# One more piece of the maxima beside an output product, and plain steps with one piece less, in a two-attention kernel

## The chip, the cores and the metric

The kernel runs on one core of one Trainium2 chip. The metric is the device time of one execution in microseconds; the number for a kernel is the median of several runs. The engines are TensorE (PE for its matmuls and PEld for its weight loads), VectorE (DVE), ScalarE (ACT), GpSimd (POOL) and the DMA queues, most of which SyncE (SP) issues.

## What is computed

Two attention layers on inputs of their own, both with 2048 positions, width 576, 32 heads of 18 and one projection each for q, k, v and for the output. Layer A looks, at each position, at 8 positions in steps of 2 back; layer B is full attention. The results stand side by side in the output.

```python
# A: W, dil = 8, 2; idx = pos - off, masked where negative
logits = einsum("bhsd,bhswd->bhsw", q, kg) * scale      # kg, vg: the 8 gathered positions
a = einsum("bhsw,bhswd->bhsd", softmax(logits), vg) @ wo_a
# B
scores = einsum("bhqd,bhkd->bhqk", q, k) * scale
b = einsum("bhqk,bhkd->bhqd", softmax(scores), v) @ wo_b
out = concatenate([a, b], axis=-1)
```

## The kernel before

**Projections, then steps.** A first part projects the inputs (and begins with the maxima). The main loop (from L1122) then makes 512 steps, numbered by `step`: 8 groups of 4 heads, in each 4 blocks of 512 queries, in each 16 tiles of 128 keys. The sixth group begins with step 320.

**A step.** For each of the 4 heads a `score` (L222): one matmul of the tile's keys with the block's queries into a PSUM bank (L229), and its exponent on ScalarE (L235). Then `weigh` (L698) multiplies the values with the exponents of the step before into `po` (L700, eight pairs of weight load and matmul to a step); after the last key tile of a block `finish` copies `po` out (L709). Heads 0 and 2 use rows 0 to 63 of the TensorE array, heads 1 and 3 rows 64 to 127. I call the four scores s0 to s3.

**Pieces of the maxima.** The softmax of B needs the largest score of each query before the block's own steps. So the scores are computed twice: ahead of time, in 2048 pieces of 128 queries by 512 keys. A piece is one matmul (`take`, L159) and one reduction on VectorE (`reduce`, L166). Each block of 64 pieces must be done several steps before the block's first score (`AHEAD`); `least`, `turn`, `halve` and `place` carry its result into the queries' rows. `maximum(r)` issues the next piece of row half r, and `given` counts the pieces by half. A score with a piece beside it (`also`) takes the piece from the other row half. I call the pieces beside scores m0 to m3, after their score.

**How many pieces.** A step has three pieces, or four when `behind()` (L1102) finds that blocks would come late; the last steps have none, when all are given. `positions` (L1111) says beside which scores: with three, heads 0, 1, 2 or 0, 1, 3, by which half has had more.

**Product steps.** The outputs of A, and part of those of B, are multiplied by their output weights inside steps of the loop: a function in `inside` is called ahead of the third or fourth score (L1129). It calls `beside` (L987), which runs two chains of matmuls of 288 columns at once, one in each row half (13 or 14 each for A, `halves`, L266), into two banks. Two pieces are put in among them, as long as pieces are left; I call them p1 and p2, and a third one p3. Which later steps count as product steps is known beforehand in `producing`; `behind` uses it. The two sums are joined by ScalarE (a copy, L918) and VectorE (an addition, L919).

**Banks.** There are seven PSUM banks in rings: 0 to 3 are "scores", and 4, 5 and 6 are "else". The pieces take their banks from "else", in turn, by `bank()` (L80); the product takes one bank from each ring. A bank is written again only when its reader has finished. Each engine works its instructions off in the order written.

Of the kernel before, what the change touches and what calls it, by code (L numbers as in the profile page):

```python
# [22 lines left out]
NG = H // 4  # L23
NT = S // 128
NB = S // 512
# [11 lines left out]
PIECES = 2 * 4 * NB  # L37
# [6 lines left out]
GAP = 54  # L44

A_FROM = 10


def ap(t, *dims):
# [10 lines left out]
def two_attentions(ctx: ExitStack, tc, xa, wa, woa, xb, wb, wob, out):  # L60
# [16 lines left out]
    rings = {"all": list(range(7)), "scores": [0, 1, 2, 3], "else": [4, 5, 6]}  # L77
    ring = "all"

    def bank(kind=None):  # L80
        r = rings[kind or ring]
        r.append(r.pop(0))
        return p_bank.tile([128, 512], F32, name=f"bank{r[-1]}")
# [25 lines left out]
    step = 0  # L109
# [4 lines left out]
    def plan(start, pieces):  # L114
        for n, f in pieces:
            agenda[start + n].append(f)

    def due():
        for f in agenda.pop(step, []):
            f()  # L120
# [84 lines left out]
    given = [0, 0]  # L205
    projecting = True

    def maximum(r):

        n, i = divmod(given[r], PIECES)  # L210
        given[r] += 1
        if n not in blocks:
            blocks[n] = block(*divmod(n, NB))
        take, reduce = blocks[n]
        piece = (r, i // 2 // NB, i // 2 % NB, i % 2)
        ps = take(*piece)
        return lambda: reduce(ps, *piece)
# [4 lines left out]
    def score(g, b, kt, h, also, kind="scores"):  # L222

        assert (g, b) in placed
        qs, ks = sets[g % 3]
        p, r = divmod(h, 2)
        ps = bank(kind)
        at = slice(64 * r, 64 * r + 56)
        nc.tensor.matmul(ps, ks[at, p, 128 * kt : 128 * kt + 128], qs[at, b, p], start=True, stop=True)  # L229
        reduce = maximum(1 - r) if also else None  # L230

        counted[0] += 1
        early = counted[0] % 8 < 6
        e = (e_room if early else work).tile([128, 512], F32, name="e", bufs=6 if early else 2)
        nc.scalar.activation(e, ps, AF.Exp, scale=SCALE)  # L235
        if reduce:
            reduce()
        return e
# [100 lines left out]
    with (tc.tile_pool(name="x", bufs=1, side="right") as xp,  # L339
# [104 lines left out]
        if True:  # L444
# [238 lines left out]
            turns = len(work_list) - NT + 4  # L683
# [8 lines left out]
        step = 0  # L692
# [5 lines left out]
    def weigh(g, b, kt, es):  # L698
        for i in range(4):
            nc.tensor.matmul(po[32 * i : 32 * i + 19], vs[g][:, kt, 19 * i : 19 * i + 19], es[i],  # L700
                             start=kt == 0, stop=kt == NT - 1)
        if kt == NT - 1:
            finish(g, b)
# [78 lines left out]
    producing = set()  # L782
# [23 lines left out]
    def local(j):  # L806
# [64 lines left out]
        def weighted(c):  # L871
            if c == 0:
                st["o"] = work.tile([128, DH, SUB], F32, name="ao", bufs=1)
            at = wide()
            nc.gpsimd.tensor_mul(at, ap(st["lg"], (0, 2), (SUB, W), (1, SUB)), window(st["v"], c))  # L875
            nc.gpsimd.tensor_add(at[:, :, :4], at[:, :, :4], at[:, :, 4:])  # L876
            nc.gpsimd.tensor_add(at[:, :, :2], at[:, :, :2], at[:, :, 2:4])
            nc.gpsimd.tensor_add(st["o"][:, 2 * c : 2 * c + 2], at[:, :, 0], at[:, :, 1])
# [28 lines left out]
        def finished(h):  # L907
            inside.append(lambda: sums_of_a(h))

        def sums_of_a(h):  # L910
            his, los = zip(*wo["a"])
            w = his[:4], los[:4], his[4], los[4]
            cols = slice(288 * h, 288 * h + 288)
            if h == 0:
                st["y"] = ys["a", j, st["n"]] = work.tile([128, D], F32, name="y", bufs=4)
            one, two = beside("scores", *(halves(r, 0, w, st["x"], cols, slice(0, 128), True) for r in range(2)))
            y = st["y"][:, cols]
            nc.scalar.activation(y, two, AF.Copy)  # L918
            behind_scores.append(lambda: nc.vector.tensor_add(y, one, y))  # L919
# [6 lines left out]
        for c in range(DH // 2):  # L926
            pieces.append((5 + 5 * c // 2, lambda c=c: match(c)))
            pieces.append((37 + 5 * c // 2, lambda c=c: weighted(c)))
        at = A_FROM + GAP * j - 24

        at = max(at, STEPS * (at // STEPS) + 14) - A_FROM - GAP * j
        for n in range(3):
            pieces.append((at + n if j else n - 7, lambda n=n: arrange(n)))
        for n, (at, ends) in enumerate(((70, (78, 80)), (81, (87, 89)))):
            pieces.append((at, lambda n=n: get(n)))
            for h in range(2):
                pieces.append((ends[h], lambda h=h: finished(h)))
                producing.add(A_FROM + GAP * j + ends[h] + 1)
            pieces.append((ends[1] + 6, lambda n=n: load(out[p0 + 128 * n : p0 + 128 * n + 128, :D], ys["a", j, n])))
# [43 lines left out]
    inside = []  # L983
# [3 lines left out]
    def beside(kind, *both):  # L987

        sums_ = [bank(k)[:, :288] for k in (kind, None)]
        turns = [[(sums_[r], *ab, i == 0, i == len(t) - 1) for i, ab in enumerate(t)] for r, t in enumerate(both)]  # L990
        pair = kind and sum(given) + 2 <= NG * NB * PIECES * 2
        if pair:

            for r in range(2):
                turns[r].insert(6 + 4 * r, None)
        for i in range(max(map(len, turns))):
            for r in range(2):
                if i < len(turns[r]):
                    if turns[r][i]:
                        ps, a, b, start, stop = turns[r][i]  # L1000
                        nc.tensor.matmul(ps, a, b, start=start, stop=stop)  # L1001
                    else:
                        maximum(r)()
        if pair:

            rings["else"].append(rings["else"].pop(0))
        return sums_

    def sum_of(y, t, h, chunks, kind=None):

        pos, cols = slice(128 * t, 128 * t + 128), slice(288 * h, 288 * h + 288)
        both = []
        for r in range(2):
            both.append([])
            for c, (hi, lo) in enumerate(chunks):
                at = slice(64 * r, min(64 * r + 64, hi.shape[0]))
                whi, wlo = wo["b"][c]
                both[r] += [(a[at, pos], w[at, cols]) for a, w in ((hi, whi), (hi, wlo), (lo, whi))]
        one, two = beside(kind, *both)
        nc.vector.tensor_copy(y, one)  # L1020
        nc.vector.tensor_add(y, two, y)
# [59 lines left out]
    for j in range(NJ):  # L1081
        plan(A_FROM + GAP * j, local(j))
    for g in range(1, NG):
# [16 lines left out]
    total = early + rest  # L1100

    def behind():  # L1102

        most = 0
        for n in range(sum(given) // (2 * PIECES), NG * NB):
            until = NT * n - AHEAD
            more = 3 * (until - step) + 2 * sum(step <= p < until for p in producing)
            most = max(most, 2 * PIECES * (n + 1) - sum(given) - more)
        return most

    def positions(n):  # L1111

        if n == 3:
            ahead = given[1] > given[0]
            return (0, 1, 3) if ahead else (0, 1, 2)
        if n == 1:
            return (0,) if given[0] > given[1] else (1,)
        return range(4) if n > 3 else (0, 1) if n == 2 else ()
# [3 lines left out]
    while step < ALL:  # L1122
        n, kt = divmod(step, NT)
        g, b = divmod(n, NB)
        places = positions(min(4 if behind() > 0 else 3, total - sum(given)))
        es = []
        for h in range(4):

            if inside and h == (3 if 3 in places else 2):  # L1129
                inside.pop(0)()  # L1130

            es.append(score(g, b, kt, h, h in places, "else" if step == ALL - 1 and h > 1 else "scores"))
        for fs in (behind_scores, outside):
            while fs:
                fs.pop(0)()
        while waiting:
            waiting.pop(0)()
        if ready:
            weigh(*ready.pop(0))
        ready.append((g, b, kt, es))  # L1140
        due()
        if waiting:
            waiting.pop(0)()
        step += 1
# [26 lines left out]
```

## Time and profile before

| | |
|---|---|
| median of 3 runs | 1646.94 us (1646.8 to 1649.85) |
| the profiled execution | 1648.65 us, its span 1646.9 us |
| PE busy, of the span | 1635.5 us, 99% |
| DVE busy | 1395.2 us, 85% |
| ACT busy | 1222.5 us, 74% |
| POOL busy | 960.6 us, 58% |
| TensorE clock granted | 1.0 |
| the loop's first and last weigh | at 423.6 and 1636 us |

A busy time adds up all the stretches in which an engine works on something. PE's matmuls are pipelined and their ends are modelled, so a PE that is always busy may still wait; the start of a weight load or of a matmul is the sharper mark. In the timeline a row is one instruction, or several of one kind one after the other: start and length in us, engine, line, operation, and behind "idle before" what the engine waited for. A line number is that of the kernel before.

### The profile page before, as it was taken

The numbers are of one execution on the slowest core, as the hardware profiler recorded it, in microseconds if no ns is written. First come the engines' busy times: TensorE is split into PE (matmuls) and PEld (weight loads), VectorE is DVE, ScalarE is ACT, GpSimd is POOL, SyncE is SP. The second block draws the span as 40 slices with busy tenths as digits, with TensorE's granted clock in tenths as the row PEclk, the third lists the DMA queues.
The fourth block names the chain that finished last, engine by engine and source line by source line (L and its number), as shares of the span: only waits on it lengthen the run. The fifth ranks groups of instructions, "written<-read, shape, count | busy, mean of one in ns | idle before, by whom it ended". The sixth has DMA issues, their size and how long they took to land.

```text
span 1646.9 us, 33732 instructions
## 1 busy us (share of the span) xinstructions
PE 1635.5 (99%) x12906; PEld 938.5 (57%) x12906; DVE 1395.2 (85%) x2386; ACT 1222.5 (74%) x2419; POOL 960.6 (58%) x800
## 2 busy tenths in 40 slices
PE   9999999999999999999999999999999999999999
PEld 7999778999433444444344344344444344344676
DVE  5199999999899989889889889899899999898533
ACT  6424432111899998998998998998998998998544
POOL 2406642210095995994994994994995997920000
PEclk9999999999999999999999999999999999999999
DMA  8937955422616346157238225616525132034201
GB/s 235 250 116 204 256 166 139 133 89 90 95 43 105 96 135 123 68 130 137 67 90 155 88 70 143 128 64 123 132 79 117 66 107 78 21 114 136 88 37 59
DMA packets 188353, 188.22 MB, mean 114 GB/s; under 512 B 118384, under 2 KB 132208, under 8 KB 186464
## 3 DMA queue, kind: packets, MB, share of 16 engines
q1 hardware_dynamic: 183328, 174.53, 40.9%
q0 software_dynamic: 4032, 10.63, 3.1%
q8 instruction: 101, 1.65, 0.4%
q10 hardware_dynamic: 832, 0.92, 0.2%
q14 instruction: 60, 0.49, 0.1%
HBM read 113.16 MB, written 88.12 MB: 122 GB/s over the span
## 4 chain that ended last, share of the span: by engine, by line
PE 93%; DMA 4%; ACT 1%; DVE 1%; POOL 0%; issue 0%; SPq 0%; ACTq 0%; POOLq 0%
PE po L700 30%; PE bank L229 25%; PE bank L322 14%; PE bank L159 13%; PE bank L1001 7%; PE bank L259 3%; DMA den<-o 1%; DMA dqk<-olo 1%; DMA dqk<-ohi 1%; DMA first<-wb 1%; DMA raw<-xa 1%; POOL xlo L370 0%; DMA raw<-xb 0%; DMA first<-xb 0%; PE bank L976 0%
## 5 line engine op out<-in xcount | busy, mean ns | idle before, releaser
L166 DVE TENSOR_REDUCE mx<-bank 128x1 f32<-128x512 f32 x2048 | 1286.9, 683 | 145.1 <-PE bank L159 113.7
L235 ACT ACTIVATE e<-bank 128x512 f32<-128x512 f32 x2048 | 1060.2, 613 | 95.0 <-PE bank L229 57.4
L159 PE MATMUL bank<-ks,qs 54*128 54x512 f32 x2048 | 751.0, 423 | 2.5 <-DVE mx L166 2.4
L229 PEld LDWEIGHTS bank<-qs,ks 56*128 56x128 f32 x2048 | 330.0, 185 | 450.2 <-ACT e L235 424.6
L229 PE MATMUL bank<-qs,ks 56*128 56x512 f32 x2048 | 581.5, 425 | 0.0
L700 PE MATMUL po<-e,v 128*19 128x512 f32 x4096 | 539.6, 599 | 0.0
L159 PEld LDWEIGHTS bank<-ks,qs 54*128 54x128 f32 x2048 | 340.6, 184 | 15.8 <-DVE mx L166 8.8
L832 POOL TENSOR_TENSOR pr<-aq,akv 128x1024 f32<-128x1024 f32 x72 | 158.4, 2200 | 28.3 <-DMA akv<-dpart 25.8
L700 PEld LDWEIGHTS po<-e,v 128*19 128x19 f32 x4096 | 69.5, 96 | 179.7 <-issue 169.3
L875 POOL TENSOR_TENSOR pr<-lg,akv 128x1024 f32<-128x1024 f32 x72 | 158.1, 2196 | 0.6
L836 POOL TENSOR_TENSOR pr<-pr 128x1024 f32<-128x1024 f32 x64 | 152.4, 2381 | 5.0
L651 ACT ACTIVATE ohi<-bank 128x512 f32<-128x512 f32 (+1 forms) x56 | 30.5, 595 | 147.3 <-issue 115.7
L322 PE MATMUL bank<-xhi,ahi 64*128 64x512 f32 (+1 forms) x448 | 113.7, 387 | 0.0
L322 PE MATMUL bank<-xhi,alo 64*128 64x512 f32 (+1 forms) x448 | 112.2, 388 | 0.0
L322 PE MATMUL bank<-xlo,ahi 64*128 64x512 f32 (+1 forms) x448 | 110.9, 389 | 0.4 <-POOL xlo L370 0.3
L876 POOL TENSOR_TENSOR pr<-pr 128x512 f32<-128x512 f32 x72 | 92.3, 1282 | 5.6
L370 POOL TENSOR_TENSOR alo<-raw,ahi 128x512 fp32r<-128x512 f32 (+1 forms) x14 | 17.6, 1254 | 120.6 <-ACT ahi L369 86.5
L463 POOL TENSOR_TENSOR olo<-olo,ohi 128x512 fp32r<-128x512 f32 x36 | 46.2, 1295 | 68.3 <-ACT ohi L462 60.8
L322 PEld LDWEIGHTS bank<-xhi,ahi 64*128 64x128 f32 (+1 forms) x448 | 64.6, 181 | 3.7
L322 PEld LDWEIGHTS bank<-xhi,alo 64*128 64x128 f32 (+1 forms) x448 | 63.3, 182 | 3.6
L322 PEld LDWEIGHTS bank<-xlo,ahi 64*128 64x128 f32 (+1 forms) x448 | 62.0, 182 | 5.2 <-POOL xlo L370 1.6
L1001 PE MATMUL bank<-wohi,at 64*128 64x288 f32 x512 | 64.5, 297 | 0.0
(196 smaller groups left out, 1738.5 us busy)
## 6 DMA issues: line engine op xcount, KB each, us to landing
do<-n SPq DMA_DIRECT2D x28, 512.0 KB
da<-ohi SPq DMA_DIRECT2D x52, 256.0 KB
dpart<-da SPq DMA_DIRECT2D x16, 702.0 KB
akv<-dpart SPq DMA_DIRECT2D x16, 702.0 KB
out<-y SPq DMA_DIRECT2D x32, 288.0 KB
qs<-dqk SPq DMA_DIRECT2D x30, 288.0 KB
ks<-dqk SPq DMA_DIRECT2D x30, 288.0 KB
at<-dao SPq DMA_DIRECT2D x64, 128.0 KB
```

The lines of the kernel that those rows point to most:

```text
L159: nc.tensor.matmul(ps, qs[at, b, p, 128 * t : 128 * t + 128], ks[at, p, 512 * k : 512 * k + 512], start=True, stop=True)
L166: nc.vector.tensor_reduce(mx[:, r, p, t, k : k + 1], ps, axis=AX.X, op=ALU.max)
L229: nc.tensor.matmul(ps, ks[at, p, 128 * kt : 128 * kt + 128], qs[at, b, p], start=True, stop=True)
L235: nc.scalar.activation(e, ps, AF.Exp, scale=SCALE)
L259: nc.tensor.matmul(ps, a, b, start=c == i == 0, stop=c == 4 and i == 1)
L322: nc.tensor.matmul(ps, a, b, start=start, stop=stop)
L700: nc.tensor.matmul(po[32 * i : 32 * i + 19], vs[g][:, kt, 19 * i : 19 * i + 19], es[i], start=kt == 0, stop=kt == NT - 1)
L832: nc.gpsimd.tensor_mul(pr, ap(st["q"][:, 2 * c], (SUB, 2), (0, W), (1, SUB)), window(st["k"], c))
L836: nc.gpsimd.tensor_add(st["pr"], st["pr"], pr)
L875: nc.gpsimd.tensor_mul(at, ap(st["lg"], (0, 2), (SUB, W), (1, SUB)), window(st["v"], c))
L876: nc.gpsimd.tensor_add(at[:, :, :4], at[:, :, :4], at[:, :, 4:])
L1001: nc.tensor.matmul(ps, a, b, start=start, stop=stop)
```

## The change

`beside` puts in three pieces instead of two, two of them in the row half that has had fewer, at places 6, 10 and 14 of the chains. While it does, the bank that the product has taken from "else" is held out of that ring, and afterwards it is put back as the last one used. A step with three pieces into which a product falls always has the pieces beside heads 0, 1 and 3, with the product ahead of head 3. From step 328 up to 395 every odd step that is not a product step has two pieces instead of three, and `behind` reckons with all that.

```diff
+TWO_FROM = 5 * NT * NB + 8
+TWO_UNTIL = TWO_FROM + 68
...
-        pair = kind and sum(given) + 2 <= NG * NB * PIECES * 2
-        if pair:
-
-            for r in range(2):
-                turns[r].insert(6 + 4 * r, None)
+        three = kind and sum(given) + 4 <= NG * NB * PIECES * 2
+        if three:
+
+            less = int(given[0] >= given[1])
+            for r, i in ((less, 6), (1 - less, 10), (less, 14)):
+                turns[r].insert(i, None)
+
+            held = rings["else"].pop()
...
-        if pair:
-
-            rings["else"].append(rings["else"].pop(0))
+        if three:
+            rings["else"].append(held)
...
-            more = 3 * (until - step) + 2 * sum(step <= p < until for p in producing)
+            twos = len([p for p in range(max(step, TWO_FROM), min(until, TWO_UNTIL)) if p % 2 and p not in producing])
+            more = 3 * (until - step) - twos + 3 * sum(step <= p < until for p in producing)
...
-        places = positions(min(4 if behind() > 0 else 3, total - sum(given)))
+        two = TWO_FROM <= step < TWO_UNTIL and step % 2 and step not in producing
+        places = positions(min(4 if behind() > 0 else 2 if two else 3, total - sum(given)))
+        if inside and len(places) == 3:
+            places = (0, 1, 3)
...
-            if inside and h == (3 if 3 in places else 2):
+            if inside and h == (3 if len(places) == 3 else 2):
```

## The prediction

> **What bounds the kernel now.** I read the page first, then the groups by line, then the timeline of single steps. A step is one pass of the main loop: four scores (L229, s0 to s3), the pieces of the maxima beside them (L159, m), and one weigh (L700). Here are the page's busy line, its chain that ended last, and two groups by line.
>
> ```profile
> PE 1635.5 (99%) x12906; PEld 938.5 (57%) x12906; DVE 1395.2 (85%) x2386; ACT 1222.5 (74%) x2419; POOL 960.6 (58%) x800
> PE 93%; DMA 4%; ACT 1%; DVE 1%; POOL 0%; issue 0%; SPq 0%; ACTq 0%; POOLq 0%
> ...
> L166 DVE TENSOR_REDUCE mx<-bank 128x1 f32<-128x512 f32 x2048 | 1286.9, 683 | 145.1 <-PE bank L159 113.7 <-PE bank L229 21.5 <-PE bank L322 0.5
> L919 DVE TENSOR_TENSOR y<-bank,y 128x288 f32<-128x288 f32 x32 | 14.3, 447 | 0.0
> ```
>
> TensorE carries 93% of the chain. VectorE at 85% is near enough to become the next bound, so I looked at one plain step on TensorE and its weight loads (columns: start, length, engine, line).
>
> ```profile
> 1101.24 0.50 PE L229 MATMUL bank<-qs,ks 56*128 56x512 f32 x1
> 1101.25 0.73 PE L159 MATMUL bank<-ks,qs 54*128 54x512 f32 x2
> 1101.58 0.69 PE L229 MATMUL bank<-qs,ks 56*128 56x512 f32 x3
> 1102.05 0.39 PE L159 MATMUL bank<-ks,qs 54*128 54x512 f32 x1
> ...
> 1102.36 0.14 PEld L700 LDWEIGHTS po<-e,v 128*19 128x19 f32 x8 [0.36 <-issue]
> ...
> 1104.49 0.14 PEld L700 LDWEIGHTS po<-e,v 128*19 128x19 f32 x8 [0.37 <-issue]
> ```
>
> A score uses rows 0-63 or 64-127 of the array and a piece the other half, so two run at once: one slot. The slots start at 1101.24, 1101.58, about 1101.82 and 1102.05: two of them take 0.47 us, so one is 0.235. Seven matmuls need four slots, one of them half empty. The weigh starts 0.31 after the last slot, and a step is 2.13 long. A whole plain stretch agrees: eight weight loads to a step, so these 328 are 41 steps, whose starts lie 85.0 us apart, or 2.125 a step.
>
> ```profile
> L700 PEld LDWEIGHTS po<-e,v x328: 94/97/100, 645.0 to 730.0; 128*19 128x19 f32 x164
> ```
>
> ScalarE comes close behind: four exponents take 2.07 us in a row, (2.07 - 0.62)/3 = 0.48 apart, or 1.93 of a step's 2.125.
>
> ```profile
> 1101.78 2.07 ACT L235 ACTIVATE e<-bank 128x512 f32<-128x512 f32 x4
> 1101.11 0.62 ACT L235 ACTIVATE e<-bank 128x512 f32<-128x512 f32 x1
> 1101.35 0.61 PEld L229 LDWEIGHTS bank<-qs,ks 56*128 56x128 f32 x3
> ```
>
> **What the change does, counted.** I followed `given`, `behind` and `positions` by arithmetic through the 512 steps. Before: 454 plain steps of three pieces and 34 product steps (32 of A, 2 of B) of 3 + 2; no step has four. After: 33 product steps (32 of A, 1 of B) of 3 + 3, 32 plain steps of two, 423 of three and one of one; again none of four. The last piece falls in step 489 instead of 488. No matmul, reduction or transfer is added or removed; the DMAs hang on step numbers, which do not move, and `place` for the last block still comes in step 493, before 496 needs it.
>
> **Two pieces in a plain step.** Six matmuls are three slots: s0 with m, s1 with m, s2 with s3. That two scores share a slot is seen at the end of the run, where no pieces are left: four scores in two slots 0.23 apart, and the weigh 0.33 after the second.
>
> ```profile
> 1606.00 0.64 PE L229 MATMUL bank<-qs,ks 56*128 56x512 f32 x4
> ...
> 1606.23 0.40 PE L229 MATMUL bank<-qs,ks 56*128 56x512 f32 x2
> ...
> 1606.56 0.14 PEld L700 LDWEIGHTS po<-e,v 128*19 128x19 f32 x8 [0.37 <-issue]
> ```
>
> So such a step can save 0.235, to 1.89. ScalarE's 1.93 does not stop it while every other step keeps three pieces: eight exponents need 3.87, two steps 4.01. But some comes back. The s3 of a step takes the bank that the s3 before left: above, that exponent ended at 1101.11 + 0.62 = 1101.73 and the last of the three weight loads began at 1101.35 + 0.61 - 0.19 = 1101.77, without spare. After a shortened step the same exponent ends 0.235 later as seen from this step, at 1101.97, the load starts at 1102.01, and a matmul whose weights come late streams some 0.10 later (the first of a step lasts 0.50 against 0.39). The last slot then starts near 1102.12 instead of 1102.05: 0.07 lost. Gain: 0.165 for each two-piece step, 32 x 0.165 = 5.3. Four of them stand before a step whose weigh waits for the copy of po, and lose up to all of it; I take off 0.5.
>
> ```profile
> PEld po L700 <- ACT o L709: 10.1, 28, 0.4
> ```
>
> Gain 4.8; bounds 2 (ScalarE's lag adds up) and 7.5 (32 x 0.235).
>
> **The third piece in a product step.** Now the step that matters. Here is a product step of before in the form that the change gives to all of them (product ahead of s3): its two ends, the two pieces inside the product (p1, p2), the piece m3 behind it, and the reductions of p1 and p2.
>
> ```profile
> 1383.38 0.14 PEld L700 LDWEIGHTS po<-e,v 128*19 128x19 f32 x8 [0.35 <-issue]
> 1385.97 0.39 PE L159 MATMUL bank<-ks,qs 54*128 54x512 f32 x1
> 1386.44 0.46 PE L159 MATMUL bank<-ks,qs 54*128 54x512 f32 x1
> 1387.27 0.39 PE L159 MATMUL bank<-ks,qs 54*128 54x512 f32 x1
> 1387.59 0.14 PEld L700 LDWEIGHTS po<-e,v 128*19 128x19 f32 x8 [0.27 <-issue]
> 1386.39 0.69 DVE L166 TENSOR_REDUCE mx<-bank 128x1 f32<-128x512 f32 x1
> 1387.00 0.68 DVE L166 TENSOR_REDUCE mx<-bank 128x1 f32<-128x512 f32 x1
> ```
>
> The step takes 4.21. Its three banks of the ring "else" go to m0, m1 and the product's second half. Before, p1 and p2 take m0's and m1's, the ring is turned by one, and m3 takes p1's, free since 1386.39 + 0.69 = 1387.08. After, the product's bank is held out and only two are left for p1, p2, p3 and m3: p3 takes p1's, and **m3 takes p2's, which is not free before 1387.00 + 0.68 = 1387.68**. Without that wait m3 would start at 1387.27. What such a wait costs is seen where VectorE was late (the reduction, then the weight load it released; further down the last piece of another step and the weigh after it).
>
> ```profile
> 1055.19 0.63 DVE L166 TENSOR_REDUCE mx<-bank 128x1 f32<-128x512 f32 x1
> 1055.87 0.18 PEld L159 LDWEIGHTS bank<-ks,qs 54*128 54x128 f32 x1 [0.50 <-DVE mx L166]
> ...
> 1524.38 0.18 PEld L159 LDWEIGHTS bank<-ks,qs 54*128 54x128 f32 x1 [0.30 <-DVE mx L166]
> 1524.80 0.14 PEld L700 LDWEIGHTS po<-e,v 128*19 128x19 f32 x8 [0.24 <-issue]
> ```
>
> The load begins 0.05 after the reduction's end (1055.82), and the weigh 0.42 after the load. So m3 loads at 1387.73 and the weigh starts at 1388.15: a step of 4.77. Queued behind m3 on TensorE are the weigh and the whole next step; nothing passes it. p2's reduction cannot come sooner, since p1's waits for its matmul and p2's follows at 0.61. This is the case with two pieces in rows 0-63 (16 products, p1 and p2 where they were). In the other 17, p1 is in rows 64-127, which run ahead by about one matmul of the product, since s2 fills rows 0-63 as the product begins, and p2 is in rows 0-63; p2's matmul then sets the pace, and I estimate 4.73. p3 can have p1's bank at 1387.13, about when its turn comes, and m3's wait covers what it may lose. The product steps of A now take 4.24 (the first) and 4.22 (the last of 32), with the 4.21 above 4.22 in mean, so the mean rise, to (16 x 4.77 + 17 x 4.73)/33 = 4.75, is 0.53.
>
> ```profile
> 608.97 0.14 PEld L700 LDWEIGHTS po<-e,v 128*19 128x19 f32 x8 [0.36 <-issue]
> 613.21 0.14 PEld L700 LDWEIGHTS po<-e,v 128*19 128x19 f32 x8 [0.36 <-issue]
> ...
> 1506.77 0.14 PEld L700 LDWEIGHTS po<-e,v 128*19 128x19 f32 x8 [0.38 <-issue]
> 1510.99 0.14 PEld L700 LDWEIGHTS po<-e,v 128*19 128x19 f32 x8 [0.26 <-issue]
> ```
>
> 33 x 0.53 = 17.5; bounds 0.42 (13.9, the weigh right behind m3 without the late load's 0.10) and 0.58 (19.1). The next step's m0 takes p3's bank, reduced at about 1388.4, long before the m0 at 1389.1: the wait is not handed on.
>
> VectorE's load alone would not foretell this: six reductions at 0.61 and the sum at 0.45 are 4.1 of the 4.21 us. The Trainium skill, TensorEngine Tiling (Array Packing), section PSUM Bottleneck, says that tiling speeds TensorE but not the emptying of PSUM; read as a rule of throughput, 4.1 under 4.21 leaves the product step at its length, which is the first rival. Against the change speaks Perfetto Trace Analysis, section Matmuls, in the same skill: independent groups should rotate through different banks so that emptying one overlaps the next. The trace's 0.50 at 1055.87 agrees with the second.
>
> **The tail.** Steps 487 to 489 hold the same 10 pieces and the same products in twelve slots instead of eleven: +0.2, within -0.5 and +1.
>
> **Sum.** +17.5 - 4.8 + 0.2 = +12.9. The profiled execution took 1648.65 (span 1646.9 and 1.75 around it), so 1661.6 there; the median of the runs shown, 1646.94, is 1.7 lower, and against it the forecast is 1659.8. A measurement of this kernel can tell about 0.2%, 3.3 us.
>
> **Rivals.**
> - *No wait at m3 (ends faster).* If p2's bank were free by 1387.27, a product step would cost only the slot on the fuller half: 0.235 in the 16 with two pieces in rows 0-63 (14 product matmuls there against 13), nothing in the others: +3.8, less the gain of 7.5 in full, so about 1643.4. For it: VectorE's load fits, as above. Against it: p2's reduction ends 0.41 too late by its row. It decides where the wait costs under (4.8 - 0.2)/33 = 0.14 a step. Chance 0.09.
> - *A shorter wait,* 0.2 a step, because p1 and p2 come sooner than I place them: +6.6 - 4.8 + 0.2, about 1649. Against it: the form is in the trace already. 0.07.
> - *ScalarE sets the pace of the short steps:* no gain, +17.7, about 1664.6. For it: the 1.93 against 1.89; against it: the three-piece steps between. 0.07.
> - *The change does not do what it says,* and four-piece steps come back, each 4 x 0.61 = 2.44 against 2.125 on VectorE: ten would add 3, about 1663. My count says none. 0.03.
>
> **How the numbers follow.** The forecast has 0.74. Its range by the bounds is 13.9 - 7.5 to 19.1 - 2, that is 1653 to 1664; to hold eight in ten I take 1652 to 1665, which leaves out the first two rivals. Slower: 0.74 + 0.07 + 0.03, and 0.01 of the shorter wait, 0.85; same 0.06; faster 0.09.
>
> **What would show it.** Right: in the product steps the weight load of the piece behind the product has an idle time of 0.3 to 0.5 before it, ended by VectorE's L166, and steps of 4.7 to 4.8; two-piece steps near 1.89 and the three-piece steps after them near 2.2; the stretch from 1166 to 1319, with 32 short steps and 4 products, about 3 shorter. Wrong: product steps under 4.4, or pairs of plain steps in that stretch at 4.25.

## The result and the profile after

The changed kernel takes 1670.59 us in the median of 4 runs (1669.63 to 1673.67), the kernel before 1647.55 beside it; the ratio is 1.0135, 95% interval 1.012 to 1.015. It is slower by 23.0 us. I had forecast slower by 12.9, with 1665 as the end of the range. The profiled execution took 1673.67, its span is 1671.9. The lines of the program have moved by 3: the scores are L232, the pieces L162, their reductions L169, the weigh L703.

From the page, the busy line and the chain; from the groups by line, the pieces' weight loads:

```profile
PE 1657.0 (99%) x12906; PEld 952.3 (57%) x12906; DVE 1396.8 (84%) x2386; ACT 1222.7 (73%) x2419; POOL 960.7 (57%) x800
PE 94%; DMA 3%; ACT 1%; issue 1%; DVE 1%; POOL 0%; SPq 0%; POOLq 0%; ACTq 0%; DVEq 0%
...
L162 PEld LDWEIGHTS bank<-ks,qs 54*128 54x128 f32 x2048 | 341.8, 185 | 29.7 <-DVE mx L169 20.4 <-ACT vs L544 1.9 <-ACT e L238 0.7
```

No engine has more work: the counts of instructions are those of before, and VectorE's busy time is the same within 2 us. TensorE still carries the chain. What is new is time in which a piece's weight load stands waiting for VectorE: 20.4 us, against 8.8 before.

A product step after (step 208; the two ends, the piece behind the product, and the reductions of p1 and p2), from the timeline:

```profile
894.31 0.14 PEld L703 LDWEIGHTS po<-e,v 128*19 128x19 f32 x8 [0.35 <-issue]
897.27 0.69 DVE L169 TENSOR_REDUCE mx<-bank 128x1 f32<-128x512 f32 x1
897.88 0.68 DVE L169 TENSOR_REDUCE mx<-bank 128x1 f32<-128x512 f32 x1
898.61 0.18 PEld L162 LDWEIGHTS bank<-ks,qs 54*128 54x128 f32 x1 [0.30 <-DVE mx L169]
899.03 0.14 PEld L703 LDWEIGHTS po<-e,v 128*19 128x19 f32 x8 [0.24 <-issue]
```

p2's reduction ends at 897.88 + 0.68 = 898.56, m3's weights load 0.05 later, the weigh starts 0.42 after that, and the step is 4.72. The load of m3 stands 0.30 for VectorE in every one of the 32 product steps of A. Together they take 153.5 us against 136.0.

A pair of plain steps in the sixth group shows the short step:

```profile
1191.21 0.14 PEld L703 LDWEIGHTS po<-e,v 128*19 128x19 f32 x8 [0.25 <-issue]
1193.17 0.14 PEld L703 LDWEIGHTS po<-e,v 128*19 128x19 f32 x8 [0.25 <-issue]
1195.28 0.14 PEld L703 LDWEIGHTS po<-e,v 128*19 128x19 f32 x8 [0.24 <-issue]
```

The step of two takes 1.96, the step of three after it 2.11; the medians of all such steps are 1.96 and 2.12.

And here is what I had not foreseen. VectorE in step 217 and in step 281, then a row for each of four stretches around them (busy us of the engines, with the granted clock behind the engines):

```profile
918.46 0.25 DVE L736 RECIPROCAL den<-den 128x16 f32<-128x16 f32 x1 [3.29 <-DMA den<-o]
1071.24 0.25 DVE L736 RECIPROCAL den<-den 128x16 f32<-128x16 f32 x1 [3.58 <-DMA den<-o]
...
912.00:918.50 6.50, 5.45 (x39) 1.87 (x31) 2.98 (x6) 5.93 (x12) 6.26 (x6) 1.00 0.33 42
919.01:925.82 6.81, 6.51 (x25) 2.98 (x29) 4.70 (x9) 3.29 (x7) 6.42 (x7) 0.50 0.61 207
1066.00:1072.60 6.60, 4.43 (x29) 1.46 (x26) 3.02 (x7) 4.46 (x9) 6.37 (x6) 1.00 1.00 199
1072.61:1079.44 6.83, 6.83 (x28) 2.47 (x27) 4.51 (x9) 3.86 (x7) 6.52 (x7) 0.50 0.74 222
```

VectorE stands 3.29 and 3.58 us at the reciprocal of a block's denominators, whose load has not landed. The reductions queue behind it, no bank comes free, TensorE's weight loads stand still for 2.18 and 2.49 us, and TensorE then runs 6.8 us at half the clock. Steps 217 and 218 take 5.68 and 3.85, steps 281 and 282 5.99 and 3.85. Before, the same reciprocals waited 3.1 and 1.6 us, steps 217 and 281 took 5.03 and 3.52, and the clock stayed at 1.0 in the profiled execution:

```profile
908.76 0.25 DVE L733 RECIPROCAL den<-den 128x16 f32<-128x16 f32 x1 [3.11 <-DMA den<-o]
1055.02 0.25 DVE L733 RECIPROCAL den<-den 128x16 f32<-128x16 f32 x1 [1.63 <-DMA den<-o]
```

The difference of the two spans, 25.0, is then: 17.5 in the product steps of A; 2.8 in the plain steps up to 482 (the late loads add, the short steps take away); 1.6 in the tail from step 483 (487 to 489 take 4.73, 5.10 and 6.13 against 4.44, 4.34 and 5.57); and 3.1 ahead of the loop, whose first weigh is at 426.7 instead of 423.6. Nothing was changed there, and over the runs below that start varies from 422.8 to 426.3 with no relation to the edit. The profiled execution, 1673.67, is itself 3.1 above the median of the four. So I count those 3.1 as chance of this profile, though what made them is not shown; without them 21.9 are left of the 23.0.

### The profile page after: what moved, and what is told of

The parts are those of the page before. It is cut to its first block, busy times and chain, and to the rows that moved or that the text cites. A ratio compares the mean times of both kernels' runs of the same rounds, so it can differ in the third digit from the quotient of the medians.

```text
span 1671.9 us, 33721 instructions
## 1 busy us (share of the span) xinstructions
PE 1657.0 (99%) x12906; PEld 952.3 (57%) x12906; DVE 1396.8 (84%) x2386; ACT 1222.7 (73%) x2419; POOL 960.7 (57%) x800
## 4 chain that ended last, share of the span: by engine, by line
PE 94%; DMA 3%; ACT 1%; issue 1%; DVE 1%; POOL 0%; SPq 0%; POOLq 0%; ACTq 0%; DVEq 0%
PE po L703 30%; PE bank L232 25%; PE bank L325 13%; PE bank L162 13%; PE bank L1007 7%; PE bank L262 4%; DMA den<-o 1%; DMA raw<-xa 1%; DMA dqk<-ohi 1%; DMA dv<-vs 0%; POOL xlo L373 0%; DMA dqk<-olo 0%; PE bank L478 0%; PE bank L979 0%; DVE mx L169 0%
## 5 line engine op out<-in xcount | busy, mean ns | idle before, releaser
L169 DVE TENSOR_REDUCE mx<-bank 128x1 f32<-128x512 f32 x2048 | 1287.7, 683 | 162.6 <-PE bank L162 131.6
L162 PE MATMUL bank<-ks,qs 54*128 54x512 f32 x2048 | 758.9, 426 | 6.3 <-DVE mx L169 4.5
L232 PEld LDWEIGHTS bank<-qs,ks 56*128 56x128 f32 x2048 | 335.1, 186 | 458.2 <-ACT e L238 423.1
L232 PE MATMUL bank<-qs,ks 56*128 56x512 f32 x2048 | 589.4, 428 | 0.0
L703 PE MATMUL po<-e,v 128*19 128x512 f32 x4096 | 542.0, 601 | 0.0
L162 PEld LDWEIGHTS bank<-ks,qs 54*128 54x128 f32 x2048 | 341.8, 185 | 29.7 <-DVE mx L169 20.4
L703 PEld LDWEIGHTS po<-e,v 128*19 128x19 f32 x4096 | 69.6, 97 | 172.2 <-issue 161.9
```

What stands on the lines that cost most here:

```text
L162: nc.tensor.matmul(ps, qs[at, b, p, 128 * t : 128 * t + 128], ks[at, p, 512 * k : 512 * k + 512], start=True, stop=True)
L169: nc.vector.tensor_reduce(mx[:, r, p, t, k : k + 1], ps, axis=AX.X, op=ALU.max)
```

## Experiments

All ratios are to the kernel before on the same chip. In the first group it took 1651.88 there, in the second 1650.06, so ratios compare better than the absolute times in the expectations.

### Reciprocals three steps later, in the changed kernel

```diff
-        for at, f in ((1, lambda: load(den, o[DH:128:32])),
+        slack = 3 if g < NG - 1 else 0
+        for at, f in ((1 - slack, lambda: load(den, o[DH:128:32])),
...
-            later(at, f)
+            later(at + slack, f)
```

> The changed kernel, with the reciprocal of each block's denominators and all that hangs on it three steps later (steps 10, 11, 15, 20, 21, 22, 28 instead of 7, 8, 12, 17, 18, 19, 25; the load of the denominators stays at 1). Theory: the part of the loss that I had not foreseen is VectorE standing at the reciprocal of steps 217 and 281 for a load that comes late, so that TensorE waits for its banks and then runs 6.8 us at half clock. Then the long steps 217, 218, 281 and 282 (5.68, 3.85, 5.99, 3.85) go to 2.12, the granted clock stays at 1.0 throughout, and the time falls by about 10 to 1660. Rival: the extra loss is spread over the product steps or the short steps; then the time stays at 1670.

Measured: 1659.01, ratio 1.0047 (1.0032 to 1.0062). Steps 217, 218, 281 and 282 are back at 2.1, the clock is 1.0 throughout the loop, and the plain steps up to 482 sum to 952.4 instead of 962.9. The product steps are untouched at 153.3. So the late loads and the half clock are the second part of the loss, and a part of its own: 10.5 us by the steps, 11.6 by the medians. (The 1.35% of the result and the 0.47% here go by two medians of the kernel before that lie 4.3 us apart, so their difference is not the size of this part.)

### The same edit in the kernel before

> Before, with the same later reciprocals as in the run on the changed kernel. Theory: before's own steps 217 (5.03) and 281 (3.52) wait for the same loads; they go to 2.12, so about 4.3 less, 1643. Rival: the waits are covered or come back elsewhere: 1647, no change.

Measured: 1644.43, ratio 0.9957 (0.9943 to 0.9970): faster than both. Both long steps are gone. The plain steps up to 482 fall from 960.1 to 956.9, a little less than expected, since a new wait of 1.2 stands in step 421 (3.32), where VectorE now spends 1.68 us on a maximum of the local attention (from 1369.33) and the pieces' weight loads wait for it three times. With the late loads out of both kernels, the change costs 1.0047/0.9957, or 0.9%: some 15 us of 1644.

### The place of a block's loads

```diff
-            later(2 if g == NG - 1 else 5, lambda: place(mh, raw))
+            later(2 if g == NG - 1 else 10, lambda: place(mh, raw))
```

> The changed kernel, with place (the eight small loads of a finished block's maxima) 10 steps after halve instead of 5. Theory: the denominators come late because a block is finished five or six steps earlier (its place at 210 and 267 instead of 215 and 273), so that its loads and the large copies stand in another order on SyncE's queue. Five steps later the order of before is back: step 217 at about 5.0 and 281 at 3.5, no half clock, about 6 less than the changed kernel, 1664.5. Rival: the order does not matter, the transfers are slower for another reason: no change, 1670.

Measured: 1663.18, ratio 1.0074 (1.0058 to 1.0091). Step 217 takes 2.97, less than the 5.0 expected, step 281 3.49, and there is no half clock in the loop. SyncE's queue shows why. The first three rows are of the kernel before around step 210, the next three of the changed kernel, the last three of this run (start, length of the issuing, line, what is moved):

```profile
880.47 14.82 SPq L813 DMA_DIRECT2D dpart<-da  x3
895.39 6.31 SPq L732 DMA_DIRECT2D den<-o  x1
...
903.63 2.29 SPq L192 DMA_DIRECT2D qs<-mh  x4
```

```profile
887.14 14.64 SPq L816 DMA_DIRECT2D dpart<-da  x3
901.88 7.62 SPq L195 DMA_DIRECT2D qs<-mh  x4
...
916.56 0.59 SPq L735 DMA_DIRECT2D den<-o  x1
```

```profile
884.10 14.57 SPq L816 DMA_DIRECT2D dpart<-da  x3
898.77 6.75 SPq L735 DMA_DIRECT2D den<-o  x1
...
907.62 2.29 SPq L195 DMA_DIRECT2D qs<-mh  x4
```

The block's loads come when its last piece is done, not at a fixed step. With one more piece in each product step the block was done sooner (its last reduction in step 203 instead of 206), its loads began in step 210 instead of 215, and they got ahead of the denominators on a queue that the large copies had already stopped up. In step 281 the order is the other one: there the block's loads had stood between the copies and the denominators before (1025.01, 1039.01, 1053.11), and afterwards they came ahead of the copies, so that the denominators were issued right behind them and took 15 us to land. Delaying place brings both orders back. The reciprocal of step 281 waits 1.59 again, as before 1.63; step 217 comes out shorter than before's 5.03.

### Three pieces in the product and none behind it

```diff
-            less = int(given[0] >= given[1])
+            less = 1
...
         if inside and len(places) == 3:
-            places = (0, 1, 3)
+            places = (0, 1)
...
-TWO_UNTIL = TWO_FROM + 68
+TWO_UNTIL = TWO_FROM
```

(`behind` reckons with two more in a product step again.)

> Before's count of pieces: a product step has three pieces inside the product, always two of them in rows 64 to 127, and two beside s0 and s1, with the product ahead of s2 and no piece behind it; no two-piece plain steps. Theory (the wait is that of m3 for p2's bank, not the third piece in itself): nothing is left to wait, s2 and s3 share a slot, and the fuller half has 3 x 0.235 + 13 x 0.133 + 2 x 0.235 = 2.90 beside the fixed 1.18, so product steps of 4.08 and a time of about 1643, 4.5 under before. Rival (a third piece costs a product step 0.5 whatever stands behind it): product steps of 4.4 to 4.75, a time of 1653 to 1664.

Measured: 1652.83, ratio 1.0001 (0.9986 to 1.0016). The product steps take 4.24 in the median, as before with two inside (4.23), and not 4.75: a third piece inside costs nothing where no piece follows it. Such a step has five pieces in all, though, as before, and not the six of the changed kernel, so this run alone does not part the bank of m3 from the number of pieces. The saving that I had expected on top did not come. The timeline of one such step has the reason: p3's matmul starts 0.05 after p1's reduction has ended, with its weights loaded late, and so there is a short wait inside the product instead of the long one behind it.

### m3 behind the weigh

```diff
         es = []
+        late = False
...
             if inside and h == (3 if len(places) == 3 else 2):
+                late = len(places) == 3
                 inside.pop(0)()
...
-            es.append(score(g, b, kt, h, h in places, ...
+            es.append(score(g, b, kt, h, h in places and not (late and h == 3), ...
...
             weigh(*ready.pop(0))
+        if late:
+            maximum(0)()
```

> The changed kernel with the later reciprocals, and in each product step the last piece (m3) issued behind the weigh instead of beside s3; all counts the same. Theory (the weigh and the next step queue behind m3's wait for p2's bank): the weigh then starts 0.32 after s3, product steps of about 4.37 instead of 4.76, and m3 costs the next step a slot of its own, 2.36 instead of 2.12, so 0.15 a product step, 4.7 in all, less than the changed kernel with later reciprocals (1659.0): 1654. Rival (the third piece costs 0.5 through VectorE's or the row half's load): product steps stay at 4.7 and the next ones grow, 1659 or more.

Measured: 1671.75, ratio 1.0140 (1.0121 to 1.0159). The first half of the theory holds: with the same six pieces, but m3 behind the weigh, the product steps take 4.35. The second does not: the next steps take 2.92, not 2.36. The weight loads of that next step:

```profile
878.29 0.14 PEld L703 LDWEIGHTS po<-e,v 128*19 128x19 f32 x8 [0.27 <-issue]
879.28 0.19 PEld L162 LDWEIGHTS bank<-ks,qs 54*128 54x128 f32 x2 [0.85 <-DVE mx L169]
...
880.56 0.18 PEld L162 LDWEIGHTS bank<-ks,qs 54*128 54x128 f32 x1 [0.51 <-DVE mx L169]
...
881.21 0.14 PEld L703 LDWEIGHTS po<-e,v 128*19 128x19 f32 x8 [0.36 <-issue]
```

The fourth piece in a row after the weigh waits 0.51 for the bank of the first, which is m3. Three banks bear three pieces from one weigh to the next, and moving one behind the weigh only moves the wait.

### No short steps

```diff
-TWO_UNTIL = TWO_FROM + 68
+TWO_UNTIL = TWO_FROM
```

> The changed kernel with the later reciprocals, without the two-piece steps: every plain step has three, and the pieces run out at step 480 instead of 489. Theory (a short step saves 0.16): the stretch of steps 329 to 394 is 32 x 0.16 = 5.1 longer, 154.0 instead of 148.9; the nine steps without pieces before 489 give about 1.7 back; together 3.4 over the changed kernel with later reciprocals (1659.0), 1662.4. Rival (ScalarE sets the pace, the short steps give nothing): stretch unchanged, the time 1.7 under it.

Measured: 1657.52, ratio 1.0054 (1.0034 to 1.0074), not to be told from the 1.0047 with the short steps. The stretch went as expected. Here are the steps 329 to 395 (68 weighs, from that of step 328 on) of the changed kernel, of this run, and of the next experiment:

```profile
L703 PEld LDWEIGHTS po<-e,v x544: 94/97/100, 1187.1 to 1336.1; 128*19 128x19 f32 x182
```

```profile
L703 PEld LDWEIGHTS po<-e,v x544: 94/97/100, 1172.0 to 1325.6; 128*19 128x19 f32 x182
```

```profile
L703 PEld LDWEIGHTS po<-e,v x544: 94/97/100, 1203.4 to 1349.7; 128*19 128x19 f32 x182
```

149.0, 153.6 and 146.3 us: the short steps save 4.6. But the steps from 479 to 511 took 120.1 instead of 126.1, 6.0 less, where I had expected 1.7. With the pieces out of the way nine steps sooner, the steps 483 to 486, at 2.58 to 3.06 bound by VectorE, fall to about 2.0, which is 2.7 of the 6.0; 487 and 488 fall from 4.74 and 5.10 to 3.65 and 3.64, another 2.6. A piece that a short step leaves out in the sixth group has to be done at the end, and there it costs at least as much as it saved.

### The short steps alone

Before with the later reciprocals, and of the change only `two` and `twos`.

> Before with the later reciprocals and the 32 two-piece steps alone; the product steps keep 3 + 2. The pieces left out must go somewhere, and behind() makes steps 1 to 32 steps of four. Theory: the short steps save 32 x 0.16 = 5.1, and a step of four, bound by VectorE at 4 x 0.61 and by m3 waiting for m0's bank, takes 2.43 to 2.68, 10 to 18 more: 1649 to 1657 against 1644.4 for before with later reciprocals. Rival (an even count is what helps, four pieces fill four slots at no cost): 1639.

Measured: 1683.42, ratio 1.0210 (1.0189 to 1.0232). The third row above is clean of the third piece: 146.3 against 151.2 before (1166.05 to 1317.20), 4.9 us for 32 short steps, 0.153 each. But `behind` puts the 32 pieces into steps 1 to 32, and these take 2.73:

```profile
442.80 0.18 PEld L162 LDWEIGHTS bank<-ks,qs 54*128 54x128 f32 x1 [0.55 <-DVE mx L169]
443.22 0.14 PEld L703 LDWEIGHTS po<-e,v 128*19 128x19 f32 x8 [0.24 <-issue]
...
445.52 0.18 PEld L162 LDWEIGHTS bank<-ks,qs 54*128 54x128 f32 x1 [0.55 <-DVE mx L169]
445.95 0.14 PEld L703 LDWEIGHTS po<-e,v 128*19 128x19 f32 x8 [0.25 <-issue]
```

A fourth piece waits 0.55 for the first one's bank and sets the step's end, as m3 does in the changed product step: 0.61 x 32 = 19.5 us. VectorE is not what fills these steps: its four reductions need 2.44 of the 2.73, and in the steps shown it stands idle for 0.24. Another loss of some 20 us is an accident of that run's schedule: the pieces ran so far ahead that in step 74 they waited for keys that were still on their way, and the clock was halved for 17 us. The waits of that stretch:

```profile
PE bank L162 <- DMA ks<-dqk: 16.2, 3, 12.9
```

### Reciprocals two steps later, before

> Before with the reciprocals two steps later instead of three, looked at as the version to keep. Three steps later left a new wait of 1.2 in step 421. Theory: two steps are enough for both late loads (they were 2.3 and 0.8 late), and step 421 goes back to 2.1, so 1643.4. Rival: no change from three steps, 1644.4.

Measured: 1646.09, ratio 0.9976 (0.9965 to 0.9988). Step 421 still takes 2.77, and step 422 5.16. The intervals of two and of three steps (0.9943 to 0.9970) overlap, and from the first weigh to the last the profiles take 1209.5 and 1209.1 us: two steps and three are not to be told apart, and both beat the kernel before.

## Why the prediction was right and wrong

**Right: the direction, and the two large terms.** The third piece: 32 product steps of A rose by 153.5 - 136.0 = 17.5, or 0.55 each; forecast 0.53. The two kinds came out at 4.72 and 4.79 for the 4.73 and 4.77 on record. The bank is shown as the cause by the idle time before m3's weight load (0.30, ended by L169), by the run with m3 behind the weigh, where the product step goes back to 4.35 and the wait turns up in the step after, and by the step of four, where the same wait appears without any product. No run gave the ring a fourth bank, so it is not shown what the six pieces would cost without the wait. The gain of the short steps: 4.5 (952.4 against 956.9, both without the late loads), forecast 4.8. Its division was wrong, though the sum of a pair held: the short step took 1.96 and not 1.89, the step after it 2.12 and not 2.2. The late load of s3 that I had put into the following step stands in the short step itself: in 27 of the 32 the last score's weights are loaded 0.05 after the end of an exponent on ScalarE. In two, steps 369 and 371, right behind product steps, ScalarE was about 1.0 ahead of that load, and these took 1.88 and 1.89.

**Wrong: "the DMAs hang on step numbers, which do not move".** That sentence is the step that failed. `place` hangs on the end of a block's pieces. I had followed `given` far enough to see the last block's place, and not the place of the other blocks, nor what stood beside it on SyncE's queue. The loads moved by up to seven steps, and twice the denominators came later for it. Against before, the late loads with the half clock cost (962.9 - 952.4) - (960.1 - 956.9) = 7.3 us; my sum had nothing for it. This is shown by the runs with later reciprocals and by the one with the later place; the size is of one profile of each kernel.

**Mis-sized: the tail.** +1.6 instead of +0.2. I had counted slots of TensorE. In step 488, which rose most (0.76), the product now runs without pieces and takes both its banks from "else"; the pieces behind it wait 0.40 and 0.27 for VectorE to empty these banks (ended by L1025 and L1026).

**The sum.** 17.5 + 7.3 - 4.5 + 1.6 = 21.9, against 23.0 between the medians. The forecast of 12.9 would have been 21.6 with the 7.3 and the tail's 1.4.

**The rivals.** No wait at m3, and a shorter one, are refuted by the 4.72. ScalarE as the pace of the short steps, with no gain left, is refuted by the 4.9 that they save; all that it takes is the difference of 1.96 and 1.89. That four-piece steps come back: none did.

VectorE had no backlog when the product's pieces came: in 30 of the 32 product steps it stood idle before p1's reduction (0.09 in step 208). From there on it works without a break to m3's, so the wait is the ring's turn and VectorE's 0.61 for each piece together, not a lack of VectorE's time over the span, where its busy time did not change. The Trainium skill, Perfetto Trace Analysis, section Matmuls, has independent groups rotate through different banks, so that emptying one overlaps the next. The trace agrees: where the turn came back to a bank too soon, the load stood 0.30.

## What to carry to other kernels

Count the buffers of a ring before adding a member to a round: with three banks, the fourth write of a round waits for the first round's reader, and everything behind it on an in-order queue waits too, whatever the reader's average load. A change of pace moves every piece of work that is triggered by completion, so list those triggers and read, on each queue they pass, what they now stand in front of. And where an in-order engine has a small operation that waits for a transfer, give that transfer slack: three steps' patience at the reciprocal was worth 0.43%, more than any arrangement of the pieces tried here.

## What the hardware showed that I had not expected

Standstills of TensorE's weight loads of 2.18 and of 2.49 us, in steps 217 and 281, went with 6.8 us at a granted clock of 0.50 each, from 919.01 and from 1072.61 on, while one of 2.02 in the kernel before, in step 217, left the clock at 1.0 in the profiled execution. The price of a wait is therefore not steady: 0.2 us more of it went with a cost of 5.3 us (steps 217 and 218 over two plain steps) instead of 2.9 (step 217 over one). The two figures are no threshold. In the first group of runs the kernel before had mean granted clocks of 0.995 to 0.999, and its two longest executions, 1657.05 and 1657.44, had 0.995 and 0.996. With the later reciprocals all six had 0.999 or 1.0 (1641.64 to 1647.07). So the kernel before, too, seems to fall to the half clock in part of its executions, and the 7.3 above would be another number there. The Trainium skill, TensorE: Matmul & The Clock Gate, Part 1, tells of the clock falling to one half after an idle window of about 3.4 us that runs freely. The half clock agrees; the standstills that it came with were shorter than such a window here.
